# Chunked attention and a feed-forward network on one Trainium2 core: the first two blocks' attention in quarter products, one load of v a tile, another order at the start

## The chip, the core and the metric

The kernel runs on one NeuronCore of a Trainium2 chip. The core has five engines that each work through an instruction list of their own and wait for one another by semaphores: TensorE (PE; matrix products and transposes, its weight loads are listed as PEld), VectorE (DVE), ScalarE (ACT), GpSimd (POOL) and SyncE (SP), which here issues all DMAs. Operands lie in SBUF, products land in PSUM, which has eight banks of 128 partitions x 512 float32. The metric is the device time of one execution in microseconds (us), lower is better. The kernel before takes 864.01 us, the median of three runs (863.40 to 864.86).

## The reference

q, k and v have the shape (8, 8, 576, 64): batch, heads, positions, head size. Attention is done within chunks of 64 positions, and its result goes through a two-layer network.

```python
scores = scale * np.matmul(q_c, k_c.transpose(0, 1, 2, 4, 3))      # 64 x 64 a chunk and head
scores = scores - np.max(scores, axis=-1, keepdims=True)
attn = np.exp(scores)
attn = attn / (np.sum(attn, axis=-1, keepdims=True) + 1e-09)
out = np.matmul(attn, v_c)
x = out.transpose(0, 2, 1, 3).reshape(4608, 512)
h = x @ w_in                                                       # 512 -> 2048
g = np.where(h > 0.0, h, np.exp(np.minimum(h, 0.0)) - 1.0)
return g @ w_out                                                   # 2048 -> 512
```

All of it is float32.

## The kernel before, in words

The 4608 tokens are cut into nine blocks of 512, a block into four tiles of 128 tokens (two chunks, all eight heads). The attention of a block is done while the network of the block before it runs; only the four tiles of block 0 come ahead of everything. The tiles of blocks 0 and 1 go by `early_attention` (L303), those from block 2 on by `later_attention` (L347), which the change touches only in names.

The network keeps float32 accuracy by splitting both operands into a rounded high part and a low rest (`xhi`, `xlo`, `wi_hi`, `wi_lo`, `wo_hi`, `wo_lo`) and summing three products (`three`, L428). `hidden(f)` (below: H0 to H15) makes 128 of the 2048 hidden columns for 512 tokens in 12 products; `project` (P0, P1, ...) multiplies them by their rows of w_out in 12 more. The weights come once, in units (u0, u1, ...) of one column tile of w_in and, from u1 on, the row tile of w_out before it. The words of a loaded unit are rearranged and split by ACT (L140, L145, L188) and DVE (L169, L175, L181, L160), all within the pass over block 0. A unit is loaded into one of three buffers; u0 and u1 are loaded at the start, unit u + 2 as soon as L181 of unit u stands in the list, and from u3 on the load waits for that instruction because it takes its buffer.

An early tile takes ten steps, here by letters. T: eight TensorE transposes of q and of k to PSUM (L266). Copies by ACT: q as it is (L275), k into `kbd`, where the two heads of a pair stand on a block diagonal of zeros (L278, two copies of 64 partitions). S: the scores, eight products of 128 rows x 64 columns by 128 columns (L313). DVE takes the row maxima and subtracts (L319, L333), ACT takes the exponential (L337), DVE the sums, the reciprocal and the multiplication (L339 to L341, L282). A: four transposes of the attention (L286), copied by ACT (L289). V: sixteen 64 x 64 products with v (L297), which use two quarters of the array, (rows 0-63, columns 0-63) and (rows 64-127, columns 64-127). The put: ACT makes xhi, DVE makes xlo (L423, L424), or for block 1 ACT keeps x (L417). With `by_head`, used in block 1's tiles, ACT takes the exponential in eight instructions, one a head, that also sum (L327), and DVE does less. v is loaded in four pieces of 64 KB a tile (`load_v`, L224), q and k in one piece of 256 KB each.

The order of every engine's list is written out by hand. `LOADS` (L691) is the order of the first loads, `START` (L692) that of the first steps: a digit advances that tile by a step, `r` and `d` advance the preparation of the units, `wN` gives TensorE N transposes of an identity with no use but to keep it busy. `FIRST_BLOCK` (L696) does the same for each group of four column tiles of the pass over block 0: `H`, `e`, `P` are the network, `a` a step of the next tile.

Of the kernel before, what the change touches and what calls it, by code (L numbers as in the profile page):

```python
# [20 lines left out]
def kernel(  # L21
# [53 lines left out]
    ps_h = ctx.enter_context(tc.tile_pool(name="ps_h", bufs=2, space=bass.MemoryType.PSUM))  # L75
# [4 lines left out]
    k_apart = const.tile([P, NK, 2, P], F32, name="k_apart")  # L80
# [70 lines left out]
    def split_units():  # L151
# [13 lines left out]
        for u in range(NU):  # L165
# [13 lines left out]
            if u:  # L179
                yield from subtract(u - 1)  # L180
# [8 lines left out]
            yield  # L189
        yield from subtract(NU - 1)  # L190
# [10 lines left out]

    def chunk_of(n: int):
        b, s = divmod(n, S)
        return b, slice(s, s + C)
# [18 lines left out]

    def load_v(n0: int, pool):  # L224

        v_sb = pool.tile([P, NK, 2, D], F32, name="v_sb")
        for j in range(2):
            for c in range(2):
                b, ss = chunk_of(n0 + c * C)
                nc.sync.dma_start(  # L230
                    out=v_sb[j * C:(j + 1) * C, :, c, :],
                    in_=v[b, j::2, ss, :].rearrange("h s d -> s h d"),
                )
        return v_sb
# [25 lines left out]


    def front_tensor(q_sb, k_sb, kbd, at, psum):
        def transpose(src):
            ps = psum([P, NK, P])
            for hp in range(NK):
                nc.tensor.transpose(  # L266
                    out=ps[:, hp, :], in_=src[:, 2 * hp:2 * hp + 2, :], identity=ident
                )
            return ps

        q_ps = transpose(q_sb)
        k_ps = transpose(k_sb)
        yield
        qT = at.tile([P, NK, P], F32, name="qT")
        nc.scalar.copy(out=qT, in_=q_ps)  # L275
        for j in range(2):
            js = slice(j * D, (j + 1) * D)
            nc.scalar.copy(out=kbd[js, :, j, :], in_=k_ps[js])  # L278
        yield qT

    def back_tensor(a, z, v_sb, at, psum):
        nc.vector.tensor_tensor(out=a, in0=a, in1=z.broadcast_to([P, H, C]), op=ALU.mult)  # L282
        yield
        a_ps = psum([P, NK, P])
        for hp in range(NK):
            nc.tensor.transpose(out=a_ps[:, hp, :], in_=a[:, 2 * hp:2 * hp + 2, :], identity=ident)  # L286
        yield
        aT = at.tile([P, NK, P], F32, name="qT")
        nc.scalar.copy(out=aT, in_=a_ps)  # L289
        yield  # L290
        x_ps = psum([P, NK, P])
        for hp in range(NK):
            for c in range(2):
                cs = slice(c * C, (c + 1) * C)
                for j in range(2):
                    js = slice(j * D, (j + 1) * D)
                    nc.tensor.matmul(  # L297
                        x_ps[js, hp, cs], lhsT=v_sb[js, hp, c, :], rhs=aT[js, hp, cs],
                        start=True, stop=True,
                    )  # L300
        return x_ps

    def early_attention(tt: int, front, v_sb, kbd, at, psum, put, by_head: bool = False):  # L303

        next(front)
        yield
        qT = next(front)
        yield
        s_ps = psum([P, H, C])
        for hp in range(NK):  # L310
            for c in range(2):
                cs = slice(c * C, (c + 1) * C)
                nc.tensor.matmul(  # L313
                    s_ps[cs, 2 * hp:2 * hp + 2, :], lhsT=qT[:, hp, cs], rhs=kbd[:, hp, :, cs],
                    start=True, stop=True,
                )
        yield
        mx = sm.tile([P, H, 1], F32, name="mx")
        nc.vector.tensor_reduce(out=mx, in_=s_ps, axis=AX.X, op=ALU.max)  # L319
        a = at.tile([P, H, C], F32, name="a")  # L320
        z = sm.tile([P, H, 1], F32, name="z")
        if by_head:

            nc.vector.tensor_scalar_mul(mx, mx, -SCALE)
            yield
            for h in range(H):
                nc.scalar.activation(  # L327
                    out=a[:, h, :], in_=s_ps[:, h, :], func=AF.Exp, scale=SCALE,
                    bias=mx[:, h, :], accum_out=z[:, h, :],
                )  # L330
            yield
        else:
            nc.vector.tensor_tensor(  # L333
                out=a, in0=s_ps, in1=mx.broadcast_to([P, H, C]), op=ALU.subtract
            )
            yield
            nc.scalar.activation(out=a, in_=a, func=AF.Exp, scale=SCALE)  # L337
            yield
            nc.vector.tensor_reduce(out=z, in_=a, axis=AX.X, op=ALU.add)  # L339
        nc.vector.tensor_scalar_add(z, z, 1e-9)  # L340
        nc.vector.reciprocal(z, z)  # L341
        x_ps = yield from back_tensor(a, z, v_sb, at, psum)
        yield
        put((slice(None), slice(None), slice(tt * P, (tt + 1) * P)), x_ps)
        yield

    def later_attention(tt: int, qk, v_sb):  # L347

# [406 lines left out]
    with (  # L759
# [5 lines left out]
        for kbd in kbds:  # L765
            nc.gpsimd.memset(kbd, 0.0)
# [252 lines left out]
```

## Time and profile before

| what | us |
|---|---|
| median of three runs (lowest, highest) | 864.01 (863.40, 864.86) |
| the profiled execution's own time | 868.06 |
| its span, from its first to its last instruction | 866.3 |
| TensorE busy in the span | 847.7 (98%) |
| VectorE, ScalarE, GpSimd busy | 508.9, 484.5, 217.4 |
| granted TensorE clock, mean over the span | 0.994 of full speed |

Of the 866.3 us of span TensorE is busy for 847.7. In the forty slices of the page its busy share is 9 tenths or more from the third slice on but for two 8s (one of them the last slice), and 7 tenths in each of the first two, that is, in the first 43 us. The profiled execution is some 4 us longer than the median of the three timed ones; differences within it are taken as they are.

Times in the rows below count from the start of the span. Matmuls overlap in the array: a product's listed duration is longer than the distance to the next one's start.

### The profile page before, as it was taken

How to read it: one execution, taken by the hardware profiler on the slowest of the kernel's cores; microseconds unless marked ns; L12 is line 12 of the kernel's file. 1: busy time of each engine (PE TensorE's matmuls, PEld its weight loads, DVE VectorE, ACT ScalarE, POOL GpSimd, SP SyncE). 2: the span in 40 equal slices, each digit the busy share in tenths (PEclk: the TensorE clock that was granted, in tenths of full speed). 3: DMA queues.
4: the chain of work that ended last, by engine and by line, in shares of the span. 5: the costliest groups of instructions: out<-in, count | busy, mean ns of one | idle time of the engine just before them, and what ended most of it. 6: DMA issues, size and time to landing. Idle time of an engine off the chain costs nothing.

```text
span 866.3 us, 17307 instructions
## 1 busy us (share of the span) xinstructions
PE 847.7 (98%) x6622; PEld 732.8 (85%) x6622; DVE 508.9 (59%) x840; ACT 484.5 (56%) x933; POOL 217.4 (25%) x184
## 2 busy tenths in 40 slices
PE   7799999999999999999989999999999999999998
PEld 6678888888888888888878888888888988889997
DVE  5789996556766566456534674457556754542222
ACT  6799985344534346546635564556544645465443
POOL 2000003126223023224312242225222522252221
PEclk9899999999999999999999999999999999999999
DMA  7786552546467758887688868887869798557521
GB/s 192 198 256 198 186 151 74 163 127 198 151 220 227 222 171 252 255 241 222 196 254 265 249 214 260 258 253 222 279 202 271 214 289 271 191 195 240 171 86 49
DMA packets 156707, 180.47 MB, mean 208 GB/s; under 512 B 67024, under 2 KB 123344, under 8 KB 156624
## 3 DMA queue, kind: packets, MB, share of 16 engines
q1 hardware_dynamic: 156624, 179.36, 67.6%
q8 instruction: 52, 0.85, 0.4%
q14 instruction: 31, 0.25, 0.1%
HBM read 147.85 MB, written 24.12 MB: 199 GB/s over the span
## 4 chain that ended last, share of the span: by engine, by line
PE 90%; DMA 4%; SPq 2%; ACT 2%; DVE 1%; issue 0%; ACTq 0%
PE o L431 44%; PE h L431 41%; DMA st<-in_moe_w_out_dram 2%; PE ps_a L364 2%; DMA wi_hi<-a_dram 2%; PE ps_a L406 1%; SPq L219 1%; SPq L230 1%; PE ps_a L297 0%; PE ps_a L313 0%; SPq L119 0%; PE ps_a L266 0%; ACT st L140 0%; DMA y<-y 0%; ACT st L145 0%
## 5 line engine op out<-in xcount | busy, mean ns | idle before, releaser
L655 POOL TENSOR_TENSOR wi_lo<-e,wi_hi 128x512 fp32r<-128x512 f32 x84 | 108.6, 1293 | 331.5 <-ACT wi_hi L651 331.5
L431 PE MATMUL h<-xhi,wi_hi 128*128 128x256 f32 (+1 forms) x704 | 189.7, 315 | 0.0
L639 DVE TENSOR_TENSOR kept<-h,kept 128x256 f32<-128x256 f32 x144 | 60.9, 423 | 178.2 <-PE h L431 112.3
L634 ACT COPY kept<-h 128x256 f32<-128x256 f32 x192 | 70.2, 366 | 169.2 <-PE h L431 169.1
L431 PE MATMUL o<-wo_lo,wi_hi 128*128 128x512 f32 x384 | 152.5, 397 | 0.0
L431 PE MATMUL o<-wo_hi,wi_hi 128*128 128x512 f32 x384 | 152.3, 397 | 0.0
L431 PE MATMUL o<-wo_hi,wi_lo 128*128 128x512 f32 x384 | 149.7, 390 | 0.0
L431 PE MATMUL h<-xlo,wi_hi 128*128 128x256 f32 (+1 forms) x448 | 147.2, 329 | 0.0
L431 PEld LDWEIGHTS h<-xhi,wi_hi 128*128 128x128 f32 x704 | 124.0, 189 | 14.5 <-issue 0.3
L431 PE MATMUL h<-xhi,wi_lo 128*128 128x256 f32 (+1 forms) x448 | 131.4, 330 | 0.5 <-DVE wi_lo L160 0.5
L431 PEld LDWEIGHTS h<-xlo,wi_hi 128*128 128x128 f32 x448 | 84.5, 189 | 12.2 <-DVE xlo L424 0.2
L431 PEld LDWEIGHTS h<-wi_lo,wi_hi 128*128 128x128 f32 x576 | 81.8, 189 | 11.2 <-DMA wi_hi<-a_dram 2.2
L431 PEld LDWEIGHTS h<-xhi,wi_lo 128*128 128x128 f32 x448 | 79.7, 188 | 11.5 <-DVE wi_lo L160 0.9
L646 DVE SCALAR_TENSOR_TENSOR e<-e,kept 128x512 f32<-128x512 f32 x96 | 66.9, 697 | 36.2 <-ACT e L644 21.2
L431 PE MATMUL h<-wi_lo,wi_hi 128*128 128x256 f32 x576 | 85.0, 283 | 2.2 <-DMA wi_hi<-a_dram 2.0
L431 PEld LDWEIGHTS o<-wo_hi,wi_lo 128*128 128x128 f32 x384 | 72.3, 188 | 16.4 <-POOL wi_lo L655 0.3
L643 ACT ACTIVATE e<-kept 128x512 f32<-128x512 f32 x96 | 60.6, 632 | 34.7 <-DVE kept L639 34.6
L651 ACT CAST wi_hi<-e 128x512 fp32r<-128x512 f32 x96 | 59.8, 623 | 32.0 <-DVE e L646 31.6
L431 PE MATMUL o<-wo_hi,ghi 128*128 128x512 f32 x192 | 76.3, 397 | 0.0
L431 PEld LDWEIGHTS o<-wo_lo,wi_hi 128*128 128x128 f32 x384 | 73.8, 192 | 2.3
L507 POOL TENSOR_TENSOR kept<-wi_hi,wi_lo 128x512 f32<-128x512 f32 x16 | 20.8, 1323 | 216.7 <-DVE qT L358 132.6
L431 PEld LDWEIGHTS o<-wo_hi,wi_hi 128*128 128x128 f32 x384 | 72.7, 189 | 2.6
(100 smaller groups left out, 1379.7 us busy)
## 6 DMA issues: line engine op xcount, KB each, us to landing
wi_hi<-a_dram SPq DMA_DIRECT2D x128, 448.0 KB, 5.7
wi_lo<-a_dram SPq DMA_DIRECT2D x64, 448.0 KB, 5.5
kept<-in_q_dram SPq DMA_DIRECT2D x100, 128.0 KB, 7.2
kept<-in_k_dram SPq DMA_DIRECT2D x100, 128.0 KB, 4.9
st<-in_moe_w_in_dram SPq DMA_DIRECT2D x16, 512.0 KB, 4.2
st<-in_moe_w_out_dram SPq DMA_DIRECT2D x16, 512.0 KB, 4.9
a_dram<-kept SPq DMA_DIRECT2D x16, 512.0 KB, 4.3
y<-y SPq DMA_DIRECT2D x224, 32.0 KB, 1.9
```

The lines of the kernel that those rows point to most:

```text
L219: nc.sync.dma_start(out=dst[p0:p0 + n], in_=src[b, :, s0:s0 + n, :].rearrange("h s d -> s h d"))
L230: nc.sync.dma_start(out=v_sb[j * C:(j + 1) * C, :, c, :], in_=v[b, j::2, ss, :].rearrange("h s d -> s h d"),)
L364: nc.tensor.matmul(scores[halves[c], j, hp, :], lhsT=qT[halves[j], hp, halves[c]], rhs=kT[halves[j], hp, halves[c]], start=True, stop=True,)
L406: nc.tensor.matmul(x_ps[halves[j], c, hp, :], lhsT=v_sb[halves[c], 2 * hp + j, :], rhs=turned[halves[c], j * NK + hp, :], start=True, stop ...
L431: nc.tensor.matmul(ps, lhsT=a, rhs=b, start=start, stop=stop, skip_group_check=onto)
L507: nc.gpsimd.tensor_tensor(out=out, in0=a, in1=b, op=op)
L634: nc.scalar.copy(out=out, in_=self.x)
L639: nc.vector.tensor_tensor(out=out, in0=self.y, in1=self.kept[kept], op=ALU.add)
L643: nc.scalar.activation(out=e, in_=c, func=AF.Relu, scale=-1.0)
L646: nc.vector.scalar_tensor_tensor(out=e, in0=e, scalar=-1.0, in1=c, op0=ALU.add, op1=ALU.max)
L651: nc.scalar.copy(out=ghi, in_=e)
L655: engine.tensor_tensor(out=glo, in0=e, in1=ghi.bitcast(F32), op=ALU.subtract)
```

## The change

`early_attention` is written anew, in the layout that `later_attention` has. A tile holds one PSUM tile of two banks throughout (`both`), and `k` is copied as it is, in one copy of 128 partitions, so the zeroed `kbd` and its GpSimd memsets go. S becomes sixteen products of 64 x 64 x 64 (`score`) over all four quarters of the array in turn. A becomes sixteen 64 x 64 products with a quarter of the identity in place of four transposes of 128 x 128. V keeps sixteen 64 x 64 products, now over all four quarters (`multiply_v`). v is loaded like q and k, in one transfer a tile. At the start, tiles 2 and 3 take the exponential by head. `LOADS` and `START` are new. The PSUM tiles of the network (`ps_h`) are opened only after the start has given its eight banks back, where before two banks were theirs from the beginning.

```diff
-    LOADS = "q0 k0 q1 k1 k2 q2 u0 q3 k3 v3 v0 u1 v2 v1"
-    START = (
-        "w13 0 0 1 1 0 1 0 2 1 0 2 2 0 r 3 0 1 d 2 3 3 2 1 2 0 0 3 2 0 r 1 w7 3 d 2 r 1 "
-        "2 3 r w1 d 3 3 d d 1 d 1 3 2 w8 3 r r d w1 d d d"
+    LOADS = "q0 k0 q1 k1 q2 k2 u0 v0 q3 k3 v1 v2 v3 u1"
+    BY_HEAD = (2, 3)
+    START = (
+        "w13 0 0 1 1 0 0 2 1 1 0 2 r r d 0 2 2 1 d 3 0 0 3 1 3 3 2 0 0 d 1 1 2 3 1 1 2 2 d 3 "
+        "2 2 r r d w4 3 3 3 d 3 r r d d d d"
...
+    quarters = [(0, 0), (1, 1), (0, 1), (1, 0)]
+    def score(scores, qT, kT):
         for hp in range(NK):
             for j, c in quarters:
                 nc.tensor.matmul(
                     scores[halves[c], j, hp, :], lhsT=qT[halves[j], hp, halves[c]],
                     rhs=kT[halves[j], hp, halves[c]], start=True, stop=True,
                 )
+    def multiply_v(x_ps, v_sb, aT):
+        for hp in range(NK):
+            for c, j in quarters:
+                nc.tensor.matmul(
+                    x_ps[halves[j], c, hp, :], lhsT=v_sb[halves[c], 2 * hp + j, :],
+                    rhs=aT[halves[c], j * NK + hp, :], start=True, stop=True,
+                )
...
+        qT = at.tile([P, NK, P], F32, name="qT")
+        for i, to in enumerate((qT, kT)):
+            nc.scalar.copy(out=to, in_=both[:, i, :].rearrange("p (h t) -> p h t", h=NK))
...
+        turned_ps = both[:, 0, :].rearrange("p (h t) -> p h t", h=H)
+        for h in range(H):
+            for half in halves:
+                nc.tensor.matmul(
+                    turned_ps[half, h, :], lhsT=a[half, h, :], rhs=ident[half, half],
+                    start=True, stop=True,
+                )
...
-        psum = psum_of(ps_start)
-        front = front_tensor(loaded[f"q{tt}"], loaded[f"k{tt}"], kbds[tt], start, psum)
+        tiles = [early_attention(
+            tt, *[loaded[f"{kind}{tt}"] for kind in "qkv"],
+            start.tile([P, NK, P], F32, name="kT"), start, ps_start, split_first_x, tt in BY_HEAD,
+        ) for tt in range(NTT)]
...
+    ps_h = ctx.enter_context(tc.tile_pool(name="ps_h", bufs=2, space=bass.MemoryType.PSUM))
...
-        tc.tile_pool(name="ps_early", bufs=2, space=bass.MemoryType.PSUM))
+        tc.tile_pool(name="ps_early", bufs=1, space=bass.MemoryType.PSUM))
```

The instruction lists show what stands where. On TensorE, the last twelve rows of the start, from V of tile 0 to the first product of H0, before (L297 is V, L286 is A, L677 are the transposes with no use):

```order
L297 MATMUL ps_a_305<-qT_303,v_sb_142 64x64 x16
L286 MATMUL ps_a_327<-ident_84,a_278 128x128 x4
L286 MATMUL ps_a_335<-ident_84,a_237 128x128 x4
L677 MATMUL h_340<-ident_84 128x128 x7
L297 MATMUL ps_a_356<-qT_351,v_sb_150 64x64 x16
L677 MATMUL h_378<-ident_84 128x128
L286 MATMUL ps_a_385<-ident_84,a_324 128x128 x4
L297 MATMUL ps_a_395<-qT_354,v_sb_155 64x64 x16
L297 MATMUL ps_a_415<-qT_390,v_sb_137 64x64 x16
L677 MATMUL h_434<-ident_84 128x128 x8
L677 MATMUL h_453<-ident_84 128x128
L431 MATMUL h_494<-xhi_88,wi_hi_97 128x512
```

And now, from the transposes of tile 3's k to the first product of H0 (L274 is T, L319 is A, L252 is S, L260 is V, L650 has no use; ps_a_155, 167, 200 and 265 belong to tiles 0 to 3):

```order
L274 MATMUL ps_a_265<-ident_81,k_sb_126 128x128 x4
L319 MATMUL ps_a_155<-ident_81,a_197 64x64 x16
L252 MATMUL ps_a_265<-kT_140,qT_292 64x64 x16
L260 MATMUL ps_a_155<-qT_290,v_sb_122 64x64 x16
L319 MATMUL ps_a_167<-ident_81,a_227 64x64 x16
L260 MATMUL ps_a_167<-qT_367,v_sb_128 64x64 x16
L319 MATMUL ps_a_200<-ident_81,a_259 64x64 x16
L260 MATMUL ps_a_200<-qT_414,v_sb_130 64x64 x16
L650 MATMUL ps_a_441<-ident_81 128x128 x4
L319 MATMUL ps_a_265<-ident_81,a_317 64x64 x16
L260 MATMUL ps_a_265<-qT_462,v_sb_132 64x64 x16
L403 MATMUL h_531<-xhi_85,wi_hi_94 128x512
```

V and A of the four tiles now alternate, each A directly ahead of another tile's V; the transposes with no use fall from 17 to 4, and none stands directly ahead of H0.

On ScalarE, the stretch that ends with the last of the four xhi before (L423 is xhi, L140 and L145 are the first steps of a unit, st_147 is u1, L289 the copy after A, L188 the high part of the weights, L337 the exponential):

```order
L423 CAST xhi_88<-ps_a_305 128x4x128
L145 ACTIVATE st_131<-st_131 128x512
L337 ACTIVATE a_324<-a_324 128x512
L289 COPY qT_351<-ps_a_327 128x512
L140 ACTIVATE st_147<-st_147 128x1024
L289 COPY qT_354<-ps_a_335 128x512
L145 ACTIVATE st_147<-st_147 128x1024
L188 CAST wi_hi_97<-y_349 128x4x128
L289 COPY qT_390<-ps_a_385 128x512
L423 CAST xhi_88<-ps_a_395 128x4x128
L423 CAST xhi_88<-ps_a_356 128x4x128
L423 CAST xhi_88<-ps_a_415 128x4x128
```

And now, from tile 2's exponential to the last xhi (L297 is the exponential by head, L394 xhi, L326 the copy after A, L187 the high part of u0; st_134 is u1, L139 and L144 its first steps):

```order
L297 ACTIVATE a_259,z_260<-ps_a_200,mx_257 128x64 x8
L394 CAST xhi_85<-ps_a_155 128x2x4x64
L187 CAST wi_hi_94<-y_263 128x4x128
L326 COPY qT_367<-ps_a_167 128x512
L297 ACTIVATE a_317,z_318<-ps_a_265,mx_315 128x64 x8
L394 CAST xhi_85<-ps_a_167 128x2x4x64
L326 COPY qT_414<-ps_a_200 128x512
L394 CAST xhi_85<-ps_a_200 128x2x4x64
L139 ACTIVATE st_134<-st_134 128x1024
L144 ACTIVATE st_134<-st_134 128x1024
L326 COPY qT_462<-ps_a_265 128x512
L394 CAST xhi_85<-ps_a_265 128x2x4x64
```

The four xhi are spread out, two groups of eight exponentials stand between them, and both steps of u1 stand ahead of tile 3's last copy and xhi.

On SP, from the load of u0 (st_131) to that of u2 (st_381), before (st_147 is u1; v_sb_142 is v of tile 0):

```order
L119 DMA st_131<-in_moe_w_in_dram 128x4x256
L219 DMA q_sb_133<-in_q_dram 128x8x64
L219 DMA k_sb_135<-in_k_dram 128x8x64
L230 DMA v_sb_137<-in_v_dram 64x4x64 x4
L230 DMA v_sb_142<-in_v_dram 64x4x64 x4
L119 DMA st_147<-in_moe_w_in_dram 128x4x256
L126 DMA st_147<-in_moe_w_out_dram 128x1024
L230 DMA v_sb_150<-in_v_dram 64x4x64 x4
L230 DMA v_sb_155<-in_v_dram 64x4x64 x4
L119 DMA st_381<-in_moe_w_in_dram 128x4x256
L126 DMA st_381<-in_moe_w_out_dram 128x1024
```

And now (u0 is st_120, u1 st_134, u2 st_347; v_sb_122 is v of tile 0):

```order
L118 DMA st_120<-in_moe_w_in_dram 128x4x256
L216 DMA v_sb_122<-in_v_dram 128x8x64
L216 DMA q_sb_124<-in_q_dram 128x8x64
L216 DMA k_sb_126<-in_k_dram 128x8x64
L216 DMA v_sb_128<-in_v_dram 128x8x64
L216 DMA v_sb_130<-in_v_dram 128x8x64
L216 DMA v_sb_132<-in_v_dram 128x8x64
L118 DMA st_134<-in_moe_w_in_dram 128x4x256
L125 DMA st_134<-in_moe_w_out_dram 128x1024
L118 DMA st_347<-in_moe_w_in_dram 128x4x256
L125 DMA st_347<-in_moe_w_out_dram 128x1024
```

Sixteen v issues are four, and that of tile 0 now stands ahead of q and k of tile 3; u1 has moved behind all of v.

## Rows read from the trace of the kernel before

**Rows 1.** The page's chain that ended last, its shares by engine.
```profile
PE 90%; DMA 4%; SPq 2%; ACT 2%; DVE 1%; issue 0%; ACTq 0%
```
**Rows 2.** TensorE's timeline: start, duration, line, operands, count, idle before.
```profile
24.60 2.20 PE L297 MATMUL ps_a<-qT,v_sb 64*64 64x64 f32 x32 [3.19 <-DMA v_sb<-in_v_dram]
...
32.29 0.47 PE L431 MATMUL h<-xhi,wi_hi 128*128 128x512 f32 x1
...
35.73 0.66 PE L266 MATMUL ps_a<-ident,q_sb 128*128 128x128 f32 x4 [0.38 <-DMA q_sb<-in_q_dram]
36.71 0.63 PE L266 MATMUL ps_a<-ident,k_sb 128*128 128x128 f32 x4 [0.32 <-DMA k_sb<-in_k_dram]
...
40.80 1.09 PE L313 MATMUL ps_a<-k_apart,qT 128*64 128x128 f32 x16 [0.72 <-issue]
```
**Rows 3.** TensorE's waits from 30 to 200 us: total, times, longest.
```profile
PE h L431 <- DVE wi_lo L160: 0.5, 1, 0.5
```
**Rows 4.** SP's timeline, DMA issues: start, duration, line, transfer, count.
```profile
6.26 0.90 SPq L119 DMA_DIRECT2D st<-in_moe_w_in_dram  x1
...
7.75 1.34 SPq L219 DMA_DIRECT2D k_sb<-in_k_dram  x1
9.14 7.63 SPq L230 DMA_DIRECT2D v_sb<-in_v_dram  x8
...
38.05 3.68 SPq L230 DMA_DIRECT2D v_sb<-in_v_dram  x4
```
**Rows 5.** DMA issues at 6.5 and 8 us: KB, us from issue to landing.
```profile
st<-in_moe_w_in_dram SPq DMA_DIRECT2D x1, 512.0 KB, 5.9
...
k_sb<-in_k_dram SPq DMA_DIRECT2D x1, 256.0 KB, 6.2
```
**Rows 6.** ScalarE's timeline in the first column tiles.
```profile
36.37 0.59 ACT L448 ACTIVATE e<-h 128x512 f32<-128x512 f32 x1
...
39.53 1.17 ACT L278 COPY k_apart<-ps_a 64x512 f32<-64x512 f32 x2
...
43.32 0.31 ACT L327 ACTIVATE a<-ps_a,mx 128x64 f32<-128x64 f32 x1 [0.17 <-DVE mx L324]
...
45.73 0.65 ACT L456 CAST ghi<-e 128x512 fp32r<-128x512 f32 x1
```
**Rows 7.** Groups by line and shape, 0 to 60 us: count, busy, mean ns.
```profile
L140 ACT ACTIVATE st<-st 128x1024 f32<-128x1024 f32 x6 | 6.9, 1145 | 4.2 <-DMA st<-in_moe_w_out_dram 4.2
...
L289 ACT COPY qT<-ps_a 128x512 f32<-128x512 f32 x5 | 2.9, 578 | 0.6 <-PE ps_a L286 0.6
...
L282 DVE TENSOR_TENSOR a<-a,z 128x512 f32<-128x512 f32 x5 | 3.5, 693 | 0.2
```
**Rows 8.** The chain that ended last, in order of time: start, us, what.
```profile
42.43 5.10 DMA st<-in_moe_w_out_dram
...
51.70 2.57 PE h L431 x10
...
58.29 2.72 PE h L431 x12
...
67.36 1.02 PE ps_a L313 x16
...
74.05 0.44 PE ps_a L286 x4
74.48 2.77 PE o L431 x12
...
79.98 1.08 PE ps_a L297 x32
81.06 2.95 PE o L431 x12
...
140.97 0.62 PE ps_a L364 x32
```
**Rows 9.** Stretches of 5 us: busy times, granted clock (PEclk), DMA share, GB/s.
```profile
25.00:30.00 5.00, 5.00 (x74) 4.55 (x75) 2.52 (x3) 3.12 (x5) 0.00 (x0) 0.50 0.81 261
```

More of the change, by code (lines that the diff above doesn't have):

```diff
@@ L189, in split_units @@
             yield
+            if u == 0:
+                yield from subtract(0)
         yield from subtract(NU - 1)
@@ L222, in load_heads @@
         return dst
[L224 to L234, printed above, removed]
     def load_tokens(n0: int, qk):
@@ L253, in load_tokens @@
             "p (i h u e d) -> p i h u e d", i=2, h=NK, u=U, e=2)[:, :, :, :, 0, :]
[L262 to L345, printed above, removed]
@@ L347, in later_attention @@
-    def later_attention(tt: int, qk, v_sb):
-        halves = [slice(i * C, (i + 1) * C) for i in range(2)]
-        quarters = [(0, 0), (1, 1), (0, 1), (1, 0)]
-        qT = at.tile([P, NK, P], F32, name="qT")
-        kT = k_apart.rearrange("p h j t -> p (h j) t")[:, :NK, :]
-        for i, to in enumerate((qT, kT)):
-            nc.vector.transpose(out=to.rearrange("p h (t u) -> p h u t", u=4), in_=qk[:, i])
-            yield
-        banks[:] = [ps_a.tile([P, 2, DM], F32, name="ps_a")]
-        scores = banks[0][:, :, :NK * C].rearrange("p j (h t) -> p j h t", h=NK)
+    halves = [slice(i * C, (i + 1) * C) for i in range(2)]
@@ L368, in later_attention @@
+    def later_attention(tt: int, qk, v_sb):
+        qT = at.tile([P, NK, P], F32, name="qT")
+        kT = k_turned
+        for i, to in enumerate((qT, kT)):
+            nc.vector.transpose(out=to.rearrange("p h (t u) -> p h u t", u=4), in_=qk[:, i])
+            yield
+        banks[:] = [ps_a.tile([P, 2, DM], F32, name="ps_a")]
+        scores = first_halves(banks[0])
+        score(scores, qT, kT)
         yield
@@ L760 @@
         tc.tile_pool(name="start", bufs=NTT) as start,
-        tc.tile_pool(name="ps_start", bufs=6, space=bass.MemoryType.PSUM) as ps_start,
+        tc.tile_pool(name="ps_start", bufs=NTT, space=bass.MemoryType.PSUM) as ps_start,
     ):
         make_identity(nc, ident)
-        kbds = [start.tile([P, NK, 2, P], F32, name="kbd") for _ in range(NTT)]
-        for kbd in kbds:
-            nc.gpsimd.memset(kbd, 0.0)
         loaded = {}
@@ L813, in split_next @@
         for kt in range(NK):
-            split_x((slice(None), kt), xf[:, kt, :])
+            nc.scalar.copy(out=xhi[:, kt], in_=xf[:, kt])
+            nc.vector.tensor_tensor(
+                out=xlo[:, kt], in0=xf[:, kt], in1=xhi[:, kt].bitcast(F32), op=ALU.subtract)
     combining, loading, pairs_begun = combine(), load_operands(), 0
```

111 lines of the change are left out of this document (73 added, 38 removed).

## The prediction

> **What bounds the kernel now.** I read the chain of waits first. TensorE holds 90% of it [rows 1], and in the order of time its last stretch that is not TensorE ahead of the later blocks ends at 51.70 us, where H3 goes on [rows 8]. From there to the end of block 0 the chain is TensorE alone, product after product. So a us saved on ScalarE, VectorE or a queue after 51.7 us is worth nothing by itself, and the change is worth what it does to two things: the moment at which TensorE can run without a gap, and the length of the attention's own products between the network's. Everything after block 0 keeps its code and moves with it.
>
> The timeline of TensorE shows the gaps. V of the second tile waited 3.19 us for v; H0 began at 32.29; then the transposes of tile 4 waited 0.38 and 0.32 us for q and k, and S of tile 4 stood 0.72 us [rows 2] until ScalarE had copied its k, 39.53 + 1.17 = 40.70 [rows 6]. H3 stood another 0.5 us for the low part of u3's weights [rows 3]. VectorE reaches that only after it has begun u4, and u4 landed at 42.43 + 5.10 = 47.53 [rows 8], because eight v issues, the last four of them alone 3.68 us [rows 4], stood ahead of it on SP. 0.38 + 0.32 + 0.72 + 0.5 = 1.9 us of gaps after H0 is what could go there.
>
> **The products of a tile in block 0.** A block of 64-column products also delays the product behind it; twelve products take 2.72 us when undisturbed, 2.77 behind A, 2.95 behind V [rows 8]. S: 1.02 + 0.2 before; the same scores as 64 x 64 x 64 in four quarters are in the trace already, in the later tiles, 0.62 + 0.2 [rows 8]. Gain 0.4. V: 1.08 + 0.23 becomes the form of four quarters too, 0.62 + 0.23; gain 0.46. A: 0.44 + 0.05 before. The new A is sixteen 64 x 64 products that use only the two quarters on the diagonal, both writing one bank: exactly what the old V does, so 1.08 + 0.23; loss 0.82. Bounds of A: as fast as four quarters, 0.85 (then a tile gains 0.5), or, if the two quarters took turns, 2.2 + 0.2; the old V had the same two quarters and one bank, so I take its 1.31. Sum of a tile: -0.4 - 0.46 + 0.82 = -0.04. Four such tiles lie in block 0: **-0.1 us**, practically nothing.
>
> The Trainium skill, TensorEngine Tiling (Array Packing), Key Properties, says that changing the tiling mode drains the engine. It speaks against this edit: the old A stayed in the 128 x 128 mode and the new one leaves it and returns. The trace agrees as far as it goes (2.95 against 2.77 us behind such a block, [rows 8]); without that the four tiles would gain 4 x 0.18 = 0.7 us more.
>
> **The start, up to H0.** The copies of k lose one ScalarE instruction a tile, and the v issues shrink: eight took 7.63 us [rows 4]. So v no longer decides, and the 3.19 us wait goes. What is late next? I follow the new lists link by link. u0 was issued at 6.26 and landed 5.9 later, at 12.2; k of tile 3 was issued at 7.75 and landed 6.2 later, at 13.95 [rows 4, 5]. Two loads of 256 KB thus took 0.9 us each behind u0; now v of tile 0 stands between, so k of tile 3 lands near 12.2 + 3 x 0.9 = 14.9. Its transposes take 0.5 more (0.63 with their tail, [rows 2]); A of tile 0 stands behind them on TensorE: 15.4. (Its other input, by way of u0's first steps and the sums on VectorE, is ready near 15.0: it does not decide.) A takes 1.1: 16.5.
>
> From here ScalarE and what it waits for make one chain. A copy is 0.58 us [rows 7] and starts some 0.5 after another; eight exponentials by head take 45.73 - 43.32 = 2.41 [rows 6]; a VectorE pass over 512 takes 0.69, a unit step over 1024 takes 1.15 on ScalarE, 1.05 from start to start [rows 7]. Three copies 1.5, tile 2's exponentials 2.4, xhi of tile 0 0.6: 21.0. On VectorE xlo and L180 1.4: 22.4; L187, the copy after A, tile 3's exponentials, xhi, the next copy, 0.5 + 0.5 + 2.4 + 0.5 + 0.6: 26.9. V of tile 2, 0.7: 27.6. xhi, both steps of u1, the copy, 0.5 + 1.05 + 1.05 + 0.6: 30.8. V of tile 3 0.7, xhi 0.6, xlo 0.7, and the handovers 0.2: **33.0**. H0 now also waits for that xlo, since its PSUM bank is one of tile 3's. It began at 32.29 before, so the long start gains nothing: the wait for v goes, and two tiles' exponentials by head (1.9 us more each on ScalarE) and u1 ahead of tile 3 take its place. H0's twelve products take 2.7 [rows 8] and the tail of the last 0.4: its result is there at 36.1.
>
> **From H0 to the end of block 0.** ScalarE's first elu instruction began at 36.37, because it stood behind a step of u3 that had waited for the load. Now u2 and u3 are loaded behind four v issues and not sixteen; with H0 done at 36.1 it can start near 36.3, 0.1 earlier. Up to the copies of tile 4's q and k ScalarE's list is the same but for one copy fewer, 0.59: these end at 40.70 - 0.7 = 40.0. q and k of tile 4 have landed by then, T and H1 fit ahead of it (36.1 + 0.9 + 2.7 = 39.7). S of tile 4 begins 0.7 us earlier: **-0.7**. The wait of H3 goes: u4 no longer stands behind eight v issues, so its step on ScalarE starts as soon as ScalarE is there, 2 us before; TensorE comes 0.3 earlier only, -0.7 - 0.4 + 0.8. **-0.5**. What is late next in block 0 is ScalarE, which already decides when S of tile 4 begins; with a copy fewer a tile it has more room than before, so I cost that at nothing. After block 0 nothing changes but the PSUM tile of the early tiles, one of two banks instead of two of one; its reader is done a microsecond ahead of the next tile's transposes, as now.
>
> **The sum.** -0.1 - 0.7 - 0.5 = -1.3 us, on an execution of 868.06 us, which is 4 us above the median of 864.01. The same gain taken from the median gives **862.7 us**, 0.15% less. A measurement of this kernel can tell about 0.2%, 1.7 us, from no change, so this is a "same", close to the border of "faster".
>
> **Rivals.**
> 1. The start is shorter than my sum. It has some twenty links in 17.6 us, each taken at full length; for it speaks that ScalarE stands idle for several of them (some 1.4 us at L187 alone), so an earlier u0 or tile 3 moves all. Against it: half of it is ScalarE work that no wait shortens. H0 1.5 us earlier carries through, ScalarE's elu with it: 862.7 - 1.5 = 861.2. From 0.45 us on it counts as faster.
> 2. The clock. Before, TensorE stood for 3.19 us at 21.4 [rows 2] and then ran from 25 to 30 us at a granted 0.50, the 1.2 GHz level [rows 9], with V and the useless transposes filling the time up to H0. By my times it stands again for 3 us (20.5 to 23.6) and then has gaps up to H0, with 4 fillers for 17. If H0 runs at the low level, it takes 2.7 us more, and S of tile 4 with it: 862.7 + 2.7 = 865.4. Within 0.2% still.
> 3. Slower: the low clock outlasts H0. The same mechanism, decided by whether the level is still low when H0 is over: then T (0.9) and H1 (2.7) double as well, 862.7 + 2.7 + 3.6 = 869.0; from the first third of H1 on it is over 865.7. Against it: H0, T and H1 leave no gap, and before, the level came back within such a dense stretch.
> 4. Nothing gained: the quarters do not overlap in the early tiles as they do in the later ones, S and V stay at their price (+0.86 a tile), or ScalarE's lag returns at H3: about 864.
>
> **How the numbers follow.** My forecast 0.43, rival 1 0.27, rival 2 0.13, rival 3 0.06, rival 4 0.11. My forecast has its own spread of about 1 us from the handovers; a third of it lies under 862.3. Faster: 0.27 + 0.14 = 0.41. Slower: rival 3 and a part of rival 2, 0.09. Same: 0.50. For 8 in 10 the range runs from below rival 1 (with A as fast as four quarters on top, 861.2 - 1.8 would be 859.4, of which I take half) to rival 2: 860.2 to 865.5.
>
> **What would show it.** A of tiles 4 to 7 near 1.1 us and the product behind it near 0.5; S and V near 0.6; no wait of V for v; H0 starting between 32 and 34 with the last xlo as what ended the wait; the waits of tile 4's transposes gone, S of tile 4 waiting for ScalarE's copy at 40; no wait at H3. Wrong would be H0 below 31.5 or above 34, a granted clock under 0.9 in 33 to 40 us, or A in the chain at other than 1.1.

## The result: 0.18% slower, and the profile after

The changed kernel takes 864.73 us (median of 20 runs, 862.97 to 867.05) against 863.58 for the kernel before (20 runs, 861.80 to 865.68). The medians differ by 1.15 us; the comparison of the runs gives a ratio of 1.0018, 95% interval 1.0010 to 1.0025, or 1.6 us of 863.58. A repetition (e16 below) gave 1.0016 [1.0004, 1.0028]. The forecast was 862.7.

The profiled execution took 864.66 us, with a span of 862.9, less than the 866.3 of the one shown of before. That comparison misleads. In the execution of before TensorE is idle for 4.0 us where nothing was changed, between 310 and 500 us; in that of the changed kernel for 0.5. These are the rows of the two, before and after (stretch, length, then busy us of TensorE, its weight loads, VectorE, ScalarE, GpSimd; granted clock, DMA share, GB/s):

```profile
310.00:500.00 190.00, 186.01 (x1638) 164.03 (x1637) 109.37 (x194) 98.98 (x197) 55.57 (x43) 0.99 0.79 239
```
```profile
310.00:500.00 190.00, 189.53 (x1669) 167.51 (x1668) 114.66 (x203) 102.20 (x202) 57.59 (x44) 1.00 0.80 244
```

So the traces are compared by where a given instruction starts. Block 1 below is the first product (S of a tile) of the pass over block 1. Two lines of TensorE's timeline before, H1 and block 1:

```profile
37.10 0.48 PE L431 MATMUL h<-xhi,wi_hi 128*128 128x512 f32 x1
...
140.90 0.69 PE L364 MATMUL ps_a<-k_apart,qT 64*64 64x64 f32 x32
```

TensorE's timeline of the changed kernel, for [rows 2]:

```profile
15.99 1.97 PE L319 MATMUL ps_a<-ident,a 64*64 64x64 f32 x32
...
24.93 1.13 PE L260 MATMUL ps_a<-qT,v_sb 64*64 64x64 f32 x32 [3.23 <-ACT qT L326]
25.84 1.92 PE L319 MATMUL ps_a<-ident,a 64*64 64x64 f32 x32
...
34.59 0.50 PE L403 MATMUL h<-xhi,wi_hi 128*128 128x512 f32 x1 [1.43 <-DVE xlo L395]
...
36.81 0.63 PE L403 MATMUL h<-xhi,wi_hi 128*128 128x512 f32 x1
...
39.03 0.60 PE L274 MATMUL ps_a<-ident,q_sb 128*128 128x128 f32 x4
...
39.83 0.48 PE L403 MATMUL h<-xhi,wi_hi 128*128 128x512 f32 x1
...
43.11 0.69 PE L252 MATMUL ps_a<-k_turned,qT 64*64 64x64 f32 x32 [0.30 <-ACT k_turned L281]
...
50.04 1.15 PE L319 MATMUL ps_a<-ident,a 64*64 64x64 f32 x32 [0.57 <-DVE a L312]
...
143.38 0.69 PE L252 MATMUL ps_a<-k_turned,qT 64*64 64x64 f32 x32
```

V of the second tile no longer waits for v but, at 24.93, for ScalarE's copy. H0 begins at 34.59, not 32.29, and waits for the last xlo. Its products reach 0.63 us each where 0.39 is normal: H0 takes 4.4 us up to the transposes of tile 4; before, 3.1 without their wait (35.73 - 0.38 - 32.29). Now they have none. H1 starts at 39.83 (before 37.10), S of tile 4 at 43.11 (40.80), block 1 at 143.38 (140.90). The lag, 2.7 us, is there when H1 starts; from H1 to block 1 the kernel takes 103.55 us, before 103.80.

The granted clock in the same stretches, for [rows 9]:

```profile
14.00:18.00 4.00, 3.02 (x36) 2.50 (x36) 3.83 (x9) 0.00 (x0) 0.00 (x0) 0.59 0.92 216
...
25.00:30.00 5.00, 4.04 (x100) 3.55 (x100) 2.17 (x5) 4.05 (x20) 0.00 (x0) 0.66 1.03 309
30.00:40.00 10.00, 7.25 (x85) 5.98 (x86) 7.47 (x10) 7.86 (x11) 0.00 (x0) 0.83 0.78 211
```

The columns are as in the two rows above; the granted clock (0.59, 0.66, 0.83) is the third from the end. 1.00 is the level of 2.4 GHz, 0.50 that of 1.2 GHz, and a mean between the two is a stretch with both. Before, it was 1.00 in 14 to 18, 0.50 in 25 to 30 and 0.98 in 30 to 40 us. Now the lower level falls on work that others wait for: A of tile 0 (1.97 us, above), V of tile 1 with A of tile 2 (1.13 and 1.92), and H0. H0 above 34 and a clock under 0.9 in 33 to 40 us (0.76) are signs of being wrong that the prediction named.

The chain of waits in order of time, for [rows 8]; columns start, us, what:

```profile
9.38 5.53 DMA k_sb<-in_k_dram
14.95 1.11 PE ps_a L274 x4
...
19.58 2.37 ACT a L297 x16
24.93 1.13 PE ps_a L260 x32
26.07 1.72 PE ps_a L319 x32
...
29.74 1.14 ACT st L139
...
34.59 4.62 PE h L403 x12
41.19 1.22 DVE y L180
43.61 1.14 DVE y L174
...
47.33 1.40 ACT a L297 x9
50.04 1.15 PE ps_a L319 x32
...
75.77 1.08 PE ps_a L319 x32
76.85 2.95 PE o L403 x12
```

The page gives TensorE 93% of the chain ([rows 1]: 90%):

```profile
PE 93%; ACT 2%; DVE 2%; SPq 1%; DMA 1%; issue 1%; DVEq 0%; ACTq 0%
```

From the landing of k of tile 3 it goes through A of tile 0, eight exponentials, V and A at the low clock and a step of the second weights on ScalarE (L139) to H0. In block 0 it runs once more off TensorE, over VectorE's steps L180 and L174 and the exponentials to A of tile 4. The waits of TensorE from 30 to 200 us, for [rows 3]: the one of H3 is gone, the one of A of tile 4 (the 0.6) is new.

```profile
PE ps_a L319 <- DVE a L312: 0.9, 2, 0.6
PE ps_a L252 <- ACT k_turned L281: 0.3, 1, 0.3
PE h L403 <- DVE xlo L782: 0.2, 1, 0.2
```

### The profile page after: what moved, and what is told of

Same layout as the page of the kernel before. It is cut to its first block, busy times and chain, and to the rows that moved or that the text cites. A ratio compares the mean times of both kernels' runs of the same rounds, so it can differ in the third digit from the quotient of the medians.

```text
span 862.9 us, 17955 instructions
## 1 busy us (share of the span) xinstructions
PE 843.2 (98%) x6961; PEld 728.3 (84%) x6961; DVE 507.0 (59%) x838; ACT 483.2 (56%) x955; POOL 212.6 (25%) x179
## 4 chain that ended last, share of the span: by engine, by line
PE 93%; ACT 2%; DVE 2%; SPq 1%; DMA 1%; issue 1%; DVEq 0%; ACTq 0%
PE o L403 45%; PE h L403 42%; PE ps_a L252 2%; PE ps_a L260 2%; PE ps_a L319 1%; SPq L216 1%; DMA k_sb<-in_k_dram 1%; ACT a L297 1%; PE ps_a L274 0%; ACT qT L326 0%; ACT e L421 0%; DVE y L180 0%; ACT e L420 0%; DVE glo L431 0%; DVE t L575 0%
## 5 line engine op out<-in xcount | busy, mean ns | idle before, releaser
L403 PE MATMUL o<-wo_lo,ghi 128*128 128x512 f32 x192 | 74.9, 390 | 0.0
```

What stands on the lines that cost most here:

```text
L403: nc.tensor.matmul(ps, lhsT=a, rhs=b, start=start, stop=stop, skip_group_check=onto)
```

## Experiments

My theory when the first runs were made: the new attention of tiles 4 to 7 gains 1.2 us as forecast; the new start loses more, by the order of its work and by the lower clock. Rivals: order alone, clock alone, or an attention that gains nothing.

Each run below has 6 to 12 executions. Its ratio is to the kernel before, executed beside it, with a 95% interval of 0.0008 to 0.0017 to either side, about 1 us. Positions come from one execution each.

**One part alone.** The first kernel has the old start and the new attention of tiles 4 to 7, the second the new start and the old attention.

```diff
 e1, e14, e19 (the same kernel three times)
-    LOADS, START, early attention of tiles 0 to 3, and its pools, of after
+    those of before
 e2, e15 (the same kernel twice)
-    early attention of tiles 4 to 7 of after
+    that of before
 e16: the changed kernel once more
```

Expected of e1:

> The start of the kernel before (its order of loads, its order of work, its products and its four pieces of v for tiles 0 to 3), with the new attention only in tiles 4 to 7. Theory (the whole loss lies in the new start; the new body gains): H0 starts near 32.3 us as before, S of tile 4 comes 0.6 us sooner by one copy less on ScalarE, the waits at H3 go, a tile costs 0.04 us less: 1 us under the kernel before, about 862.5 us (before at 863.6), with no new wait on TensorE. Rival (the new A in the body, or the one PSUM tile of two banks for all early tiles, carries part of the loss): 863.6 or more, and the trace shows waits of T or A in block 0.

Expected of e2:

> The reverse: the new start, with the old attention (block diagonal k, four transposes of the attention, four pieces of v) in tiles 4 to 7. Theory (the start loses, the body gains about 1 us): H0 at 34.6 us as in the changed kernel, then the old waits for the copies of k come back: 865.5 to 866.5 us. Rival (the body carries part of the loss): 864.7 or less.

Expected of e15:

> New start, attention of tiles 4 to 7 as in the kernel before, once more, beside the changed kernel on the same chip. Theory (read from the traces: from H1's first product to the first product of block 1 the old attention takes 103.2 us in this kernel and 103.55 in the changed one, so the new attention gains nothing): time equal to the changed kernel's within 0.8 us, both 1 to 2 us over the kernel before. Rival (the new attention gains the 1.3 us that were forecast): 1.3 us or more over the changed kernel's time.

Expected of e16:

> The changed kernel once more. Theory: granted clock 0.988 to 0.996, A of tile 0 at the low clock (1.6 to 2 us), H0 at 34.3 to 34.9, H1's first product at 39 to 40, time 1 to 2 us over the kernel before. Rival (the first result was an effect of that chip or hour): time within 0.5 us of the kernel before.

Expected of e14:

> Old start, attention of tiles 4 to 7 of the changed kernel, once more. Theory (the new attention gains 0.1 us): time within 0.5 us of the kernel before. Rival (it gains 1.2 to 1.3 us): 0.7 us or more under the kernel before.

Expected of e19:

> Old start and new attention a third time, as the comparison for the run with q and k of tile 4 ahead, and to settle whether it beats the kernel before: 0.998 to 0.9995 of its time if the new attention gains 0.5 to 1.3 us, 1.000 if it gains nothing.

Ratios to the kernel before:

| | old start | new start |
|---|---|---|
| old attention | 1 | 1.0038 [1.0026, 1.0049], 1.0022 [1.0011, 1.0032] |
| new attention | 0.9992 [0.9979, 1.0005], 0.9981 [0.9968, 0.9993], 0.9991 [0.9979, 1.0003] | 1.0018 [1.0010, 1.0025], 1.0016 [1.0004, 1.0028] |

By the means of the cells the new start costs 0.0030 (2.6 us) with the old attention and 0.0017 + 0.0012 = 0.0029 (2.5 us) with the new one. So the part that I thought harmless is the loss. The new attention gains 1.0 us with the old start and 1.1 with the new, the latter with intervals that overlap side by side (865.43 and 864.98 us). The old start with the new attention is faster than the changed kernel by 0.3%, and than the one before by 0.1%: three measurements below 1, but only one of them with its whole interval. A third pair, both without the old start's useless transposes (e7 and e10 below), shows no gain: 0.9997 with the old attention, 1.0000 with the new. So a gain of the attention is likely, not shown.

The traces agree on the start: H1 begins at 37.10, 36.35, 36.61, 37.27, 37.65 and 37.46 us with the old one, at 39.83, 38.75, 39.58 and 40.27 with the new. On the attention they agree only in part. From H1 to block 1, undisturbed, the old one takes 103.2 (e2, e15, e7 below) and the new 103.06 to 103.08 (e1, e14, e10 below) after the old start, but 103.53 and 103.55 after the new. TensorE's timeline of e15 (old attention, new start):

```profile
15.82 1.97 PE L420 MATMUL ps_a<-ident,a 64*64 64x64 f32 x32
...
40.27 0.48 PE L513 MATMUL h<-xhi,wi_hi 128*128 128x512 f32 x1
...
44.16 1.09 PE L335 MATMUL ps_a<-k_apart,qT 128*64 128x128 f32 x16 [0.90 <-ACT k_apart L300]
...
50.77 0.60 PE L308 MATMUL ps_a<-ident,a 128*128 128x128 f32 x4
...
56.80 1.15 PE L319 MATMUL ps_a<-qT,v_sb 64*64 64x64 f32 x32
```

S of tile 4 waits 0.90 us here, but A comes 6.61 us after S, without a wait; in the changed kernel 50.04 - 43.11 = 6.93, with one of 0.57. From A to V it is 6.03 us here, and 6.74 there. Where the timed 1 us comes from, the traces up to block 1 don't show. Behind block 1 TensorE's waits add up to 0.7 to 3.9 us with the old attention (before, e2, e7, e15) and to 0.2 to 1.5 with the new (after, e1, e10, e14, e16, e19). The code there is the same, and so few executions don't tell whether the gain lies there.

**One exponential a tile in the start.**

```diff
-    BY_HEAD = (2, 3)
+    BY_HEAD = ()
```

Expected of e5:

> The changed kernel with the exponentials of tiles 2 and 3 in one instruction a tile, as in tiles 0 and 1, and so with VectorE's subtraction and sum for them. Theory (the start is one chain that runs through ScalarE, where each group of eight exponentials takes 1.9 us more than one): H0 comes 2 to 3 us sooner, near 32 us, about 862.5 us unless the clock falls again at H0. Rival (VectorE, which gets 1.3 us more a tile, takes the chain over): H0 within 0.7 us of 34.6 and the time within 0.8 us of the changed kernel.

1.0009 [0.9999, 1.0019]; H0 at 34.62, as in the changed kernel, although ScalarE is through with tile 3's exponentials at 24.7 and not 27.2. A of tile 0 (15.96, 1.97 us), A of tile 3 (29.34, 1.97 us) and H0 (34.62 to 39.48) all ran at the low clock in its trace: there TensorE took what ScalarE gave. That is not the whole answer, since with the clock held up H0 comes no earlier either (e11 below).

**Work that keeps the clock up.** Useless transposes in TensorE's gaps: `f1:12` stands for twelve, into tile 1's PSUM bank, which I took to be free there.

```diff
 e3:  START with  f0:4 2 2 ... f0:8 3 ... f1:12 3 ... f2:24 1 ... f3:10 2 2 d 3 ... 3 f1:10 3 3 f1:12 d 3
 e6:  the same, but 2 f0:10 2 d 3 (behind A of tile 2, not ahead of it) ... 3 f0:8 3 3 f0:10 d 3
 e8:  only the last two, 3 f0:6 3 3 f0:10 d 3
 e7:  the kernel before without its own w7, w1, w8, w1 in the middle of START
```

Expected of e3:

> The changed kernel with 80 more useless transposes on TensorE in the gaps of the start, so that its clock is not let down (4 and 8 ahead of S and T of tiles 2 and 3, 12 behind A of tile 0, 24 behind A of tile 1, 10 behind A of tile 2, 10 and 12 around V of tile 3). Theory (the loss is the 1.2 GHz clock, once at A of tile 0 and once at H0): granted clock 1.00 from 15 to 40 us, A of tile 0 takes 1.1 and not 1.97 us, H0 starts near 33.2 and takes 2.7 and not 4.4 us; 3 us less than the changed kernel, about 861.7 us. Rival (the order of ScalarE's and VectorE's work sets H0 and the clock comes beside it): H0 still at 34 or later and the time within 0.8 us of the changed kernel.

Expected of e6:

> The changed kernel with useless 128x128 transposes in TensorE's idle stretches, none of them ahead of A of tile 2 this time. Theory (the loss is what the low clock does to the chain that ends at H0, and to H0 itself): A of tile 0 at about 1.15 us instead of 1.97, the exponentials of tile 3 from 23.1 instead of 24.8, A of tile 2 at 23.9, the last xlo ending near 32.8 instead of 34.5, H0 in 2.7 us instead of 4.2; the first products of block 1 at 140.1 instead of 143.4, and a time 1 us under the kernel before. Rival (the order of ScalarE's work sets H0 and the clock only goes along with it): H0 again at 34.5 to 35, block 1 at 141.9 to 142.3, a time 1 to 3 us over the kernel before, as the other run with such transposes.

Expected of e8:

> The changed kernel with useless transposes only just ahead of H0: six behind A of tile 3 and ten behind V of tile 3. Theory: A of tile 0 stays at the low clock and H0 still starts near 34.6, but its twelve products take 2.7 to 3 us instead of 4.2, so block 1 begins near 142 instead of 143.4: a time of 0.3 to 0.5 us over the kernel before. Rival (what counts is the start of H0 alone): H0 at 34.6 and block 1 still at 143 or later, a time as that of the changed kernel, 1.1 us over the kernel before.

Expected of e7:

> The kernel before with its own useless transposes in the middle of the start (7, 1 and 9 of them) left out, the thirteen at the very beginning kept. Theory (the change took away what held the clock up at H0): the granted clock falls to 0.50 in 33 to 37, H0's products take 0.63 instead of 0.39 us for some of them, block 1 begins 1.5 us later than 140.9 at H0's start of 32.3, time 1 to 1.5 us longer than the kernel before. Rival (the clock falls only by the changed kernel's own gaps, which are not in the kernel before): no difference, clock 0.998 as before.

e3: 1.0039 [1.0026, 1.0052], with a granted clock of 1.00 from 10 us on: a miss. Its ten transposes ahead of A of tile 2 waited 1.69 us for the exponentials whose bank they overwrote, so A came at 26.87, and H0 at 34.96. They held the clock and lost the time again by their place. e6 has them behind A; these are its A of tile 0, A of tile 2, H0, the transposes of tile 4 and H1:

```profile
15.54 1.15 PE L326 MATMUL ps_a<-ident,a 64*64 64x64 f32 x32
...
24.18 1.50 PE L326 MATMUL ps_a<-ident,a 64*64 64x64 f32 x32
...
33.20 0.47 PE L410 MATMUL h<-xhi,wi_hi 128*128 128x512 f32 x1 [0.28 <-DVE xlo L402]
...
36.05 0.60 PE L281 MATMUL ps_a<-ident,q_sb 128*128 128x128 f32 x4
...
36.85 0.48 PE L410 MATMUL h<-xhi,wi_hi 128*128 128x512 f32 x1
```

A of tile 0 takes 1.15 us, A of tile 2 starts at 24.18, H0 at 33.20 and takes 2.85; H1 begins at 36.85, as with the old start, block 1 at 140.52. The time is 1.0000 [0.9990, 1.0011]. e8 mends H0 alone:

```profile
16.05 1.97 PE L326 MATMUL ps_a<-ident,a 64*64 64x64 f32 x32
...
34.74 0.47 PE L410 MATMUL h<-xhi,wi_hi 128*128 128x512 f32 x1 [0.28 <-DVE xlo L402]
...
37.60 0.60 PE L281 MATMUL ps_a<-ident,q_sb 128*128 128x128 f32 x4
...
38.39 0.48 PE L410 MATMUL h<-xhi,wi_hi 128*128 128x512 f32 x1
```

H0 still starts at 34.74, after three A at the low clock (1.92 to 1.97 us), but takes 2.86 us: H1 at 38.39, block 1 at 142.01, 1.0010 [0.9996, 1.0024]. So of the 3.0 us between H1 in the changed kernel (39.83) and in e6 (36.85), H0's own speed is 1.4 and the low clock ahead of it 1.5. In these traces that is the whole lag of H1. In time e6 gives back 0.0017 of 0.0029 by the ratios; the rest lies partly behind H1, where it takes 103.67 us to block 1 and e1 103.08.

e7 is a miss of mine: 0.9997 [0.9985, 1.0010], H0's products at 0.39 us. The old start does not need its transposes. It also shows what was particular to the one execution shown of before:

```profile
35.04 0.63 PE L266 MATMUL ps_a<-ident,q_sb 128*128 128x128 f32 x4 [1.34 <-DMA q_sb<-in_q_dram]
...
46.74 0.60 PE L286 MATMUL ps_a<-ident,a 128*128 128x128 f32 x4
...
52.89 1.15 PE L297 MATMUL ps_a<-qT,v_sb 64*64 64x64 f32 x32
```

H0 begins at 29.97, earlier than in [rows 2], but H1 comes at 36.35, only 0.75 earlier, since q of tile 4 now keeps the transposes for 1.34 us. In the other traces with the old start it keeps them for 0.38 to 2.01 us: that load sets H1. And from A to V of tile 4 it is 6.15 us, not 54.19 - 47.40 = 6.79: H3's wait of 0.5 us [rows 3] does not come again.

**The order with the clock held up.**

```diff
 e9:   e6 with LOADS = "q0 k0 q1 k1 q2 k2 q3 k3 u0 v0 v1 v2 v3 u1"
 e11:  e6 with BY_HEAD = ()
 e12, e17 (twice): e11 with the second weights' steps moved (r, and with them some d), w4 left out
-    2 f0:10 2 d 3 2 2 r r d w4 3 f0:8 3 3 f0:10 d 3
+    2 r f0:6 2 r d 3 2 d 2 d f0:2 3 f0:8 3 3 f0:10 3
 e13:  e12 without any f
```

Expected of e9:

> As the run with transposes in all idle stretches, and q and k of tile 3 fetched ahead of the first weights and of v of tile 0. Theory: k of tile 3 lands some 0.8 us earlier, its turn has no wait, A of tile 0 at 14.6 instead of 15.1, and all up to H0 0.5 us earlier: H0 at 32.3, block 1 at 139.6, time 1.5 us under the kernel before. Rival (the first weights then come too late: their steps on VectorE wait and push the softmax of tile 0): H0 no earlier than in the run that it is set beside, same or longer time.

Expected of e11:

> As the run with useless transposes in all idle stretches, and the softmax of tiles 2 and 3 as of the first two, with one exponential a tile and the sum on VectorE. Theory (with the clock held up, the chain through the eight exponentials of tile 3 on ScalarE is what still sets H0): exponential of tile 3 done at 23.5 instead of 25.8, A of tile 3 at 27.3 instead of 28.9, the last xlo at 30.7, H0 at 31.3 instead of 33.2, block 1 at 138.6, time 1 to 1.5 us under the kernel before. Rival (VectorE, which gets the subtraction and the sum of these tiles in their place, or the loads of the second weights set H0): H0 at 33 or later, block 1 at 140.5, time as the kernel before within 0.5 us.

Expected of e12:

> The run with transposes in the idle stretches and sums on VectorE, with ScalarE's two steps for the second weights (1.16 and 1.18 us) put into its idle stretches ahead of and behind the copy of tile 2, where they stood ahead of the copy of tile 3, and six transposes instead of fourteen ahead of A of tile 3. Theory (with the clock held up, the place of these two steps on ScalarE is what sets H0): the copy of tile 3 at 29.0 instead of 30.7, H0 at 31.8 instead of 33.5, block 1 at 139.1 instead of 140.8, time 1.3 to 1.7 us under the kernel before. Rival (the steps of the second weights land on another chain, V of tile 2 or the first weights' rest on VectorE): H0 at 33 or later, time as the kernel before within 0.5 us.

Expected of e13:

> The same order without any useless transposes. Theory: A of tile 0 runs at the low clock again (1.97 us) and so all behind it comes 1.3 to 1.6 us later than in the run with the transposes, H0 at 33.2, and its products take 4 us instead of 2.7; block 1 at 142 and a time 1 to 1.5 us over the kernel before, clock 0.990 to 0.994. Rival (the order alone was the loss, the clock only goes with the idle stretches that the order left): H0 at 32 to 32.5 with products at full speed, block 1 within 0.5 us of the run with the transposes.

Expected of e17:

> The run with transposes in the idle stretches, sums on VectorE and the second weights' steps in ScalarE's idle stretches, once more. Theory: H1's first product at 34.8 to 36 against 36.4 to 37.7 with the old start, 3 to 4 us ahead of the changed kernel's; time 0.5 to 1.5 us under the kernel before and 2 to 3 under the changed kernel. Rival (its start was early in that one trace only): time as the kernel before within 0.4 us.

e9: 1.0016 [1.0007, 1.0026], the rival. k of tile 3 is no longer waited for, but A of tile 0 waits 2.23 us for VectorE, whose list has a step of the first weights ahead of it, for which ScalarE waited 1.92 us.

e11: 0.9999 [0.9991, 1.0007], the rival too, H0 at 33.50. Tile 3's exponential is done at 23.7, but its copy comes at 30.67, behind the second weights' two steps on ScalarE, which begin at 28.52 and 29.58. e12 moves those: the copy is at 28.14, H0 at 31.21 and H1 at 34.82, 2.3 us ahead of e11, 1.1 of which is k of tile 3 landing earlier in that run (its transposes start at 14.09 and 15.17). That leaves an estimated 1.2 us for the order, in this one pair of traces; the repetition does not bear it out, with H1 at 38.22. Time 0.9996 [0.9979, 1.0013], in the repetition 1.0006 [0.9994, 1.0018]: no gain that holds. The trace of the repetition shows a part of why:

```profile
25.96 1.50 PE L326 MATMUL ps_a<-ident,a 64*64 64x64 f32 x31 [2.02 <-issue]
...
34.62 0.47 PE L410 MATMUL h<-xhi,wi_hi 128*128 128x512 f32 x1 [0.28 <-DVE xlo L402]
```

A of tile 2 stops behind its first product, for 2.02 us here, 1.00 in e12 and 0.87 in e11, with "issue" as the releaser: for nothing that the profile shows. Only these three traces have it there, those with the added transposes and one exponential a tile. The other part lies far behind the start, where the code is the same in all. There V of a later tile waits for VectorE, which itself waits for a DMA: 2.20 us in e12 and 1.75 in e17, the two longest of all these traces (none in the changed kernel's first trace, 1.02 in its second). In e12:

```profile
441.86 0.69 PE L260 MATMUL ps_a<-turned,v_sb 64*64 64x64 f32 x32 [2.20 <-DVE turned L383]
```

So nearly half of the 4.9 us by which e12's block 1 (138.51) is ahead of the changed kernel's was gone again there.

e13, without them, got 1.0005 [0.9990, 1.0021]: H0 at 32.27, its products at full clock in this trace, block 1 at 139.57 against 138.51. Both theories in part: A of tile 0 (1.63 us) was slow, H0 was not. But that was one execution of three in twelve with a mean clock of 0.996; most had 0.988 to 0.994 and took longer. By the ratios one exponential a tile gives back 0.0008 of the changed kernel's 0.0017 (e5), and with this order 0.0012, both without a held clock and with intervals that overlap the changed kernel's. So the times do not separate the low clock from the order that leaves the gaps; only the positions in e6 and e8 do, and they hold for this order.

**Mending the old start.** e10 is e1 without the old transposes; e18 is e1 with q and k of tile 4 issued ahead of the next weights.

Expected of e10:

> The start of the kernel before without its useless transposes in the middle, and the attention of tiles 4 to 7 of the changed kernel. Theory (the two parts of the change stand apart: the body gives 1.2 us, the transposes of the old start give or cost nothing that can be measured): H0's second product at 31.2 or earlier, block 1 at 138.4 to 139.7, time 0.7 to 1.2 us under the kernel before, clock 0.997. Rival (the old transposes hold the clock up for H0 after all): granted clock 0.50 in part of 31 to 36, block 1 at 141 or later, time not under the kernel before.

Expected of e18:

> Old start and new attention, with q and k of tile 4 fetched ahead of the third weights instead of behind them. Theory (with the old start the turn of tile 4 waits 1.2 to 1.9 us for q and 0.35 for k, and that wait sets H1): both waits gone, H1's first product at 35.2 to 35.7 instead of 36.6 to 37.6, block 1 at 138.7, time 1 to 1.5 us under the same kernel without it. Rival (the third weights come 2.6 us later, and their steps on ScalarE and VectorE, or the copy of k of tile 4 behind them, take the place of the wait): H1 earlier but S of tile 4 or H2 later, time the same within 0.4 us.

e10: 1.0000 [0.9988, 1.0013], H1 at 37.65, block 1 at 140.71, no low clock at H0; again it is q of tile 4 (1.88 us) that is waited for. e18: 1.0021 [1.0007, 1.0036], worse than the rival: the transposes of tile 4 have no wait, but H1 itself, at 39.23, stands for the weights that were put behind them, and the time is 0.0030 above that of e19.

```profile
35.07 0.60 PE L376 MATMUL ps_a<-ident,q_sb 128*128 128x128 f32 x4
...
39.23 0.50 PE L514 MATMUL h<-xhi,wi_hi 128*128 128x512 f32 x1 [3.12 <-ACT wi_hi L188]
...
40.59 0.79 PE L514 MATMUL h<-xhi,wi_lo 128*128 128x512 f32 x1 [0.63 <-DVE wi_lo L160]
```

**The clock, run by run.** Each timed execution has its mean granted clock. Medians of the changed kernel's 32 runs: 866.19 us (9 runs up to 0.990), 864.85 (17 runs, 0.991 to 0.994), 863.43 (6 runs at 0.996). The kernel before has a median clock of 0.998, and 863.29 us over the 165 runs made beside the experiments. Where the changed kernel keeps its clock nearly as high, it is as fast.

## Why the prediction failed, step by step

The sum had three gains of 1.3 us together and a start that costs nothing. The gains came to 1.0 us by the times of two pairs, and to none by a third. The start cost 2.5.

- **The link chain up to H0 (33.0) is the step that failed: it took TensorE's links, and H0 behind them, at the full clock.** The load of k of tile 3 was right: forecast at 14.9, its transposes began at 14.95. A of tile 0 was forecast from 15.4 to 16.5, the full clock, and ran from 15.99 to 17.96; the transposes took 1.11 us where e6 has 0.66. What is behind kept the order of links that I gave, 1.4 to 1.5 us late: xhi of tile 0 ends near 22.4 (21.0), the last xlo at 34.5 (33.0). With the clock held up (e6), the same list gives H0 at 33.20 and H1 at 36.85, where my times make it 37.0 (36.1 and 0.9). So the links were right and the speed of TensorE's links was not.
- **H0 "takes 2.7": it took 4.4.** That is rival 2 in mechanism; in size 2.7 were forecast and 1.4 to 1.7 seen. I had given it 0.13, because I looked for the low clock at H0 only and priced the useless transposes as what had kept it up. e7 shows that they were not what did that. Rival 2 also missed the earlier half of the loss, which is as large (e6 and e8). On the median of 864.01 from which it was reckoned, the ratio makes 865.6; its 865.4 was the nearest of all. That is in part luck: H0 cost less than it says, the unforeseen half ahead of H0 made up for it, and the 1.3 us of gains that it starts from did not come in full.
- **Rival 3** did not come: H1 ran at full speed (0.39 to 0.40 a product from 40.14 on in the changed kernel), so no more than rival 2.
- **S of tile 4 0.7 us earlier.** From H1 to S it is 3.28 us against 3.70, a gain of 0.4. But A of tile 4 waits instead, 0.57 us, for VectorE's list. That ScalarE is what is late next in block 0 was wrong there: the chain of waits to A of tile 4 runs over VectorE's L180, L168 and L174, and then over the exponentials.
- **The wait at H3, -0.5.** It is gone, but it was one of that execution; three others with the old attention (e2, e7, e15) have none of 0.2 us or more. A term read from a single wait of 0.5 us in a single trace should not have gone into the sum.
- **The products, -0.04 a tile: right.** A takes 1.08 us, the product behind it is at 2.95 against 2.72 for twelve, V and S are at 0.62. From the transposes of tile 5 to those of 6 it is 63.15 to 88.81, 25.66 us, before 61.02 to 86.73, 25.71. The rule of the Trainium skill cited in the prediction (TensorEngine Tiling (Array Packing), Key Properties), that a change of mode drains the engine, fits these rows as before: 0.23 us behind each such block. It decided nothing.
- **v no longer decides, no wait at tile 4's transposes**: right, and worth nothing, as e7 shows for the old start: what sets H1 there is q of tile 4, and taking that away (e18) brings the next weights' wait.

What stays open: whether the new attention gains 1 us, as two pairs of times say, and where, while the traces up to block 1 show 0.15 us with the old start and a loss of 0.3 with the new; how much of the start's loss another order would give back without held clock; and what "issue" waits for in e11, e12 and e17. A load of instructions is a candidate: the page's queue for them moved a packet between 23.5 and 24.0 us in e17, where the stop begins at 23.9. But in e11 and e12 the packet lies a microsecond or more ahead of the stop, and e6 has one at 22.0 to 22.5 and no stop.

## What to carry to other kernels

When TensorE's work gets shorter or its gaps longer, price the products behind each gap at both levels of its clock, the short ones on the chain (A: 1.15 or 1.97 us here) as well as the long ones (H0: 2.9 or 4.4). Before a wait is counted as a gain, look for the list of another engine that ends within the same microsecond, and look whether the wait is in more than one execution. Two halves of a change that stand apart are tested apart: here one half cost 0.3% and the other gained 0.1% at best.

## What was not expected of the hardware

- The lower level of the clock comes and goes from run to run: A of tile 0 took 1.97 us in four traces of the new start, 1.64 and 1.63 in two, 1.15 in one, with the same code ahead of it on TensorE. The old start is not safe either: in e19, behind a wait of 2.01 us at the transposes of tile 4, H1's first six products took 0.58 to 0.77 each.
- Useless transposes held the granted clock at 1.00 from 10 to 40 us in e3, e6, e11 and e12, and yet none of these was clearly faster than the kernel before. e3 lost the time by their place; in e11's trace H0 stood behind ScalarE's steps for the second weights, and e12's has the stop and the later wait shown above. In e17 the transposes did not hold it: after the stop of 2.02 us it was 0.66 from 25 to 30 us.
- On SP's queue a load moved ahead was paid for by what it was moved past: 2.23 us of new wait in e9, 3.12 + 0.63 in e18, more than the wait that went (0.7 and 1.2 to 2.0).
